# Pooled attention and two feed-forward layers: VectorE shares the pooling of the second batch, and the first block's second product runs unsplit in all sixteen steps

## Chip, cores and metric

The kernel runs on one core of a Trainium2 chip. The metric is the device time of one execution in microseconds; lower is better. The engines are named as in the profile: PE (TensorE, matrix products), PEld (its weight loads), DVE (VectorE), ACT (ScalarE), POOL (GpSimd) and SP (SyncE, whose queue SPq issues the DMAs here). "Lnnn" is line nnn of the kernel before.

## What is computed

Pooled attention over 8 batches of 8 heads, then two feed-forward layers on the 4608 tokens (576 for each batch) of width 512, with an inner width of 2048. All inputs and the output are float32.

```python
k_p = k.reshape(B, H, Sp, pool, D).mean(axis=3)      # pool 8: 576 -> 72
v_p = v.reshape(B, H, Sp, pool, D).mean(axis=3)
scores = scale * np.matmul(q, k_p.transpose(0, 1, 3, 2))
attn = softmax(scores)
x = np.matmul(attn, v_p)                             # then heads side by side: 4608 x 512
h = x @ moe_w_in
g = np.where(h >= 1, h, np.where(h <= -1, 0, (h + 1) ** 2 / 4))
x = g @ moe_w_out
h = x @ moe2_w_in
return np.maximum(h, 0) ** 2 @ moe2_w_out
```

## The kernel before

**Blocks and steps.** The tokens are cut into nine blocks of 512 (`TB`) and 36 attention tiles of 128, four tiles to a block. In the first layer a block takes 16 steps, one for each slice of 128 of the inner width. In step s, `gemm1(s)` (L666) makes the slice's inner values ph from the block's x with 12 matrix products, `step_ops` turns ph into g, and `gemm2(s - 2)` multiplies the g of two steps before (`LAG` is 2) with a slice of `w_out` and adds into four banks acc (L727 or L738). The first block is steps 0 to 15. Its products of step s - 2 are issued right behind the first products of step s.

**Split and unsplit products.** A float32 product is made either from two parts of each operand, a high and a low one, with three products on the parts (hi x hi, hi x lo, lo x hi; `split_hi` on ACT at L219, `split_lo` on DVE at L223), or as one plain float32 product on the operands as they are. `whole("o", s)` chooses the plain form for the second product of the steps below `WHOLE`, 10 before the change. In a plain step there are four products and g is written to a tile that the trace calls gw (L699). In a split step there are twelve products, and besides them wohi (ACT, L219), wolo (DVE, L223), gh (ACT, L701) and gl (DVE, L707).

**Weights.** In the first block the weights of the first layer also arrive (st) and go through a conversion, `convert_w`: two instructions on ACT, three on DVE (L155, L158, L161), one on POOL (L164). There are 16 wi and 16 wo conversions. The program lets them run ahead of their use: behind step s, 2s + 8 are begun (`LEAD` is 8), and they are ended in the step after; 2s + 4 are ended ahead of the g of step s.

**Attention beside the steps.** The attention of the later tiles is cut into small units that are laid into half-steps (`slots`). The first four tiles, those of block 0, are done ahead of step 0. For each batch there are four k tiles and four v tiles of 72 rows by 2 heads by 8 x 64 values (`load_kv`, three buffers kv). `pool_kv` adds the eight positions of a group on DVE in halves (widths 4D and 2D, then the last one, L297 and L298) for batches 2 to 7. The first two batches (`ON_PE` is 2) are summed in the matrix products that also turn k (`unit_k`, products pk, L309) and that place v (`unit_v`, products pv, L329): for batch 1 these go through all eight positions; for batch 0 DVE first adds two halves (L286), and the products go through two positions. Batch 1 is first used by attention tile 4; its units stand in half-steps 2, 3 (k) and 7, 9 (v). The product px (L488) gives a tile of x; it needs the transposed weights of attention aT, which DVE makes (L478) from z, a tile that was stored to DRAM (pd) and fetched back.

**Order.** Every engine works through its own queue in order. The framework sets the order of each queue from the order of the program and the time at which it reckons an operand to be ready, so that a step's instructions can stand among those of a later one: in the trace two pk groups of the program's neighbouring half-steps stand 13 us apart, and some conversions run several steps early. All DMAs stand in the one queue of SP.

Of the kernel before, what the change touches and what calls it, by code (L numbers as in the profile page):

```python
# [21 lines left out]
LEAD = 8  # L22
HEADS = 3

WHOLE = 10

TURNED = 8

# [5 lines left out]
def pooled_attention_moe_moe(  # L34
# [15 lines left out]
    POOL = 8  # L50
# [44 lines left out]
    ON_PE = 2  # L95
# [136 lines left out]
    def bank(shape, name):  # L232

        n = early[-1] % 8 if early else 0
        if n >= 4:
            return ps_acc.tile(shape, F32, tag=f"acc{n - 4}", name=name)
        if n % 2:
            return ps_h.tile(shape, F32, tag="h", name=name)
        return ps_a.tile(shape, F32, tag="a", name=name)
# [39 lines left out]
        kv_t[nm, b, p] = a  # L279

    def pool_kv(nm, b, p):
        if b == 0:

            a = kv_t[nm, b, p]
            for w in (4 * D, 2 * D):
                nc.vector.tensor_tensor(out=a[:, :, 0:w], in0=a[:, :, 0:w], in1=a[:, :, w:2 * w], op=ALU.add)  # L286
        if b < ON_PE:
            return
        a = kv_t.pop((nm, b, p))
        if nm == "v":  # L290
            if p == 0:
                vp[b] = at.tile([SP, H, D], F32, tag="vp", name="vp")
            o = vp[b][:, 2 * p:2 * p + 2, :]
        else:
            o = kp[b, p] = at.tile([SP, 2, D], F32, tag="kp", name="kp", bufs=4)
        for w in (4 * D, 2 * D):
            nc.vector.tensor_tensor(out=a[:, :, 0:w], in0=a[:, :, 0:w], in1=a[:, :, w:2 * w], op=ALU.add)  # L297
        nc.vector.tensor_tensor(out=o, in0=a[:, :, 0:D], in1=a[:, :, D:2 * D], op=ALU.add)  # L298

    def unit_k(b, p0):  # L300
        pk = bank([P, 2, SP], "pk")
        for i in range(2):
            if b < ON_PE:

                a = kv_t.pop(("k", b, p0 + i)).rearrange("s h (r d) -> s h r d", r=POOL)
                n = 2 if b == 0 else POOL
                for r in range(n):
                    for e in range(2):
                        nc.tensor.matmul(  # L309
                            out=pk[e * D:(e + 1) * D, i, :], lhsT=a[:, e, r, :], rhs=ident[:SP, :SP],  # L310
                            start=(r == 0), stop=(r == n - 1),
                        )
                continue
            nc.tensor.transpose(out=pk[:, i, :], in_=kp.pop((b, p0 + i)), identity=ident[:SP, :SP])

        def evac():
            t = kbd[b % 2]
            nc.scalar.activation(out=t[0:D, p0:p0 + 2, 0:SP], in_=pk[0:D], func=AF.Copy)
            nc.scalar.activation(out=t[D:P, p0:p0 + 2, SP:2 * SP], in_=pk[D:P], func=AF.Copy)

        return evac

    def unit_v(b, p0):
        pv = bank([P, 2, 2, D], "pv")
        for i in range(2):
            a = kv_t.pop(("v", b, p0 + i)).rearrange("s h (r d) -> s h r d", r=POOL)
            n = 2 if b == 0 else POOL
            for r in range(n):
                nc.tensor.matmul(  # L329
                    out=pv[:SP, i], lhsT=ident[:SP, :SP], rhs=a[:, :, r, :],  # L330
                    start=(r == 0), stop=(r == n - 1),
                )

        def evac():
            if p0 == 0:
                vp[b] = at.tile([SP, H, D], F32, tag="vp", name="vp")
            nc.scalar.activation(
                out=vp[b][:, 2 * p0:2 * p0 + 4, :], in_=pv[:SP].rearrange("s i h d -> s (i h) d"), func=AF.Copy
            )

        return evac
# [173 lines left out]
    for t in range(TB0, NTILE):  # L515
# [10 lines left out]
        if t in first_tile:  # L526
            b = first_tile.index(t)
# [24 lines left out]
    def pool_to(n):  # L552
        while kv_pooled[0] < min(n, len(kv_order)):
            load_kv_to(kv_pooled[0] + 1)
            pool_kv(*kv_order[kv_pooled[0]])
            kv_pooled[0] += 1
            load_kv_to(kv_pooled[0] + (1 if kv_pooled[0] > 3 * NP else 2))
# [6 lines left out]
    def unit(u):  # L564
        if u[0] == "k":
            b, p = u[1:]
            pool_to(b * 2 * NP + p + 2)
            return unit_k(b, p)
        if u[0] == "v":
            b, p = u[1:]  # L570
            pool_to(b * 2 * NP + NP + p + 2)
            return unit_v(b, p)
        if u[0] == "q":
            load_q_to(u[1] + (1 if u[1] >= TB0 else 0))
            return unit_q(u[1])
        if u[0] == "s":
            return unit_s(*u[1:])
        if u[0] == "p":
            return unit_p(*u[1:])
        b = max(r[2] for r in runs(u[1] * P, P))  # L580
        pool_to((b + 1) * 2 * NP)
        return unit_x(u[1])
# [43 lines left out]
    def whole(kind, s):  # L626

        return kind == "o" and s < WHOLE

# [470 lines left out]
    for n, u in enumerate(units):  # L1100
        kind, b, i, g = u
# [52 lines left out]
```

## Time and profile before

| | us |
|---|---|
| median of three runs | 1641.57 (1641.28 to 1642.41) |
| profiled execution | 1640.99 |
| its span in the trace | 1639.2 |
| PE busy in the span | 1611.4 |
| DVE busy in the span | 1266.7 |

Busy times are sums of the durations of an engine's instructions. In the timelines the duration of a matrix product reaches over the start of the next one; how fast they follow each other is read from their start times. A plain float32 product stands in the trace as two records, as do those of pk and pv. The granted clock is given as a share of TensorE's full clock, 2.4 GHz.

### The profile page before, as it was taken

What the parts mean: (1) busy time and instruction counts of PE and PEld (TensorE: products, weight loads), DVE (VectorE), ACT (ScalarE), POOL (GpSimd) and SP (SyncE); (2) the same over time, 40 slices, a digit from 0 to 9 for tenths busy, and PEclk for the clock granted to TensorE, in tenths of its full rate; (3) what the DMA queues carried; (4) which work ended last, traced back from release to release, by engine and by line L of the source; (5) the groups of instructions that cost most, each with busy time, mean ns of one, the idle gap of its engine ahead of it and who ended that gap; (6) DMA issues with size and microseconds to landing.
All of it is one profiled execution on the core that took longest, in us unless ns stands there. A gap on an engine that the chain in (4) does not pass through costs nothing.

```text
span 1639.2 us, 23215 instructions
## 1 busy us (share of the span) xinstructions
PE 1611.4 (98%) x7776; PEld 1309.5 (80%) x7776; DVE 1266.7 (77%) x2236; ACT 893.4 (55%) x1610; POOL 104.1 (6%) x75
## 2 busy tenths in 40 slices
PE   6999999999999999999999999999999999999998
PEld 5667887888878888888888888888888878888886
DVE  7999889898898999998885452579558855975585
ACT  6665556666666666666775532345435533553353
POOL 1441000001000100000100000000000000000000
PEclk9999999999999999999999999999999999999999
DMA  9665336455454554454370284677777776768675
GB/s 243 187 190 132 87 86 178 140 154 154 133 163 138 168 148 135 149 152 161 129 270 7 96 275 148 194 218 207 194 255 218 209 229 213 211 199 246 193 207 130
DMA packets 280518, 284.69 MB, mean 174 GB/s; under 512 B 154960, under 2 KB 183632, under 8 KB 280400
## 3 DMA queue, kind: packets, MB, share of 16 engines
q1 hardware_dynamic: 280400, 283.21, 58.0%
q8 instruction: 62, 1.02, 0.3%
q14 instruction: 56, 0.46, 0.1%
HBM read 218.10 MB, written 65.01 MB: 173 GB/s over the span
## 4 chain that ended last, share of the span: by engine, by line
PE 92%; DVE 3%; DMA 2%; ACT 1%; issue 1%; SPq 0%; DVEq 0%; ACTq 0%
PE ph L666 26%; PE acc L738 25%; PE dp L1012 11%; PE cp L1003 10%; PE dq L1012 5%; PE cr L1003 5%; PE dr L1012 3%; PE cq L1003 3%; PE pss L372 2%; PE px L488 2%; DMA kv<-in_v_dram 1%; DMA st<-in_moe_w_out_dram 1%; PE acc L727 0%; DMA kv<-in_k_dram 0%; DVE wilo L223 0%
## 5 line engine op out<-in xcount | busy, mean ns | idle before, releaser
L666 PE MATMUL ph<-xhi,wihi 128*128 128x512 f32 x576 | 232.0, 403 | 2.0 <-DVE wi L158 1.9
L666 PE MATMUL ph<-xhi,wilo 128*128 128x512 f32 x576 | 226.3, 393 | 0.0
L666 PE MATMUL ph<-xlo,wihi 128*128 128x512 f32 x576 | 226.3, 393 | 0.0
L960 ACT ACTIVATE gh<-g 128x512 fp32r<-128x512 f32 x224 | 139.8, 630 | 153.0 <-DVE g L1029 47.9
L738 PE MATMUL acc<-gh,wohi 128*128 128x512 f32 x536 | 215.6, 402 | 0.0
L738 PE MATMUL acc<-gl,wohi 128*128 128x512 f32 x536 | 209.8, 391 | 0.0
L738 PE MATMUL acc<-gh,wolo 128*128 128x512 f32 x536 | 209.2, 390 | 0.0
L768 DVE TENSOR_TENSOR gl<-g,gh 128x512 fp32r<-128x512 f32 x224 | 150.9, 685 | 47.6 <-ACT gh L960 46.1
L1003 PE MATMUL cp<-x,w 128*128 128x512 f32 x768 | 186.3, 390 | 0.2
L1003 PEld LDWEIGHTS cp<-x,w 128*128 128x128 f32 x768 | 143.9, 188 | 31.3 <-ACT s L1025 1.4
L1012 PE MATMUL dp<-gh,w 128*128 128x512 f32 x512 | 161.5, 389 | 0.0
L219 ACT ACTIVATE wihi<-wi 128x512 fp32r<-128x512 f32 x144 | 90.4, 628 | 110.9 <-PE ph L666 110.0
L223 DVE TENSOR_TENSOR wilo<-wi,wihi 128x512 fp32r<-128x512 f32 x144 | 106.3, 738 | 43.8 <-ACT wihi L219 42.8
L666 PEld LDWEIGHTS ph<-xhi,wihi 128*128 128x128 f32 x576 | 109.2, 190 | 29.4 <-issue 3.2
L701 ACT ACTIVATE gh<-g 128x512 fp32r<-128x512 f32 x134 | 84.2, 628 | 82.0 <-DVE g L699 80.9
L666 PEld LDWEIGHTS ph<-xhi,wilo 128*128 128x128 f32 x576 | 109.0, 189 | 23.4 <-issue 0.2
L666 PEld LDWEIGHTS ph<-xlo,wihi 128*128 128x128 f32 x576 | 109.2, 190 | 22.0 <-issue 0.7
L707 DVE TENSOR_TENSOR gl<-g,gh 128x512 fp32r<-128x512 f32 x150 | 105.9, 706 | 23.1 <-ACT gh L701 20.1
L1025 ACT ACTIVATE s<-cp 128x512 f32<-128x512 f32 x96 | 57.1, 595 | 118.0 <-PE cp L1003 118.0
L738 PEld LDWEIGHTS acc<-gl,wohi 128*128 128x128 f32 x536 | 100.6, 188 | 22.2
L738 PEld LDWEIGHTS acc<-gh,wohi 128*128 128x128 f32 x536 | 100.7, 188 | 20.2 <-issue 0.8
L738 PEld LDWEIGHTS acc<-gh,wolo 128*128 128x128 f32 x536 | 100.8, 188 | 19.5
(142 smaller groups left out, 2997.3 us busy)
## 6 DMA issues: line engine op xcount, KB each, us to landing
w<-w2i SPq DMA_DIRECT2D x224, 256.0 KB
w<-w2o SPq DMA_DIRECT2D x224, 256.0 KB
w2i<-cb SPq DMA_DIRECT2D x32, 512.0 KB
w2o<-cb SPq DMA_DIRECT2D x32, 512.0 KB
st<-in_moe_w_out_dram SPq DMA_DIRECT2D x31, 512.0 KB
st<-in_moe_w_in_dram SPq DMA_DIRECT2D x29, 512.0 KB
pd<-pad SPq DMA_DIRECT2D x32, 384.0 KB
z<-pd SPq DMA_DIRECT2D x96, 128.0 KB
```

Source lines behind the costliest of these rows:

```text
L219: nc.scalar.activation(out=hi, in_=src, func=AF.Copy)
L223: eng.tensor_tensor(out=lo, in0=src, in1=hi.bitcast(F32), op=ALU.subtract)
L372: nc.tensor.matmul(out=pss[off:off + n, i, :], lhsT=qT[t][:, p, off:off + n], rhs=kbd[b % 2][:, p, :], start=True, stop=True,)
L666: nc.tensor.matmul(out=ph, lhsT=a[:, kk % a.shape[1], :], rhs=c[:, kk, :], start=(i == 0), stop=(i == 3 * KD - 1))
L701: act(out=gh, in_=g, func=AF.Copy)
L707: nc.vector.tensor_tensor(out=gl, in0=g, in1=gh.bitcast(F32), op=ALU.subtract)
L738: nc.tensor.matmul(out=o, lhsT=lhsT, rhs=rhs, start=(f == 0 and x == 0), stop=(f == KF - 1 and x == 2),)
L768: tt(out=out, in0=a, in1=b, op=ALU.subtract)
L960: act(out=hi, in_=a, func=AF.Copy)
L1003: nc.tensor.matmul(out=out[0], lhsT=w[:, a, k, :], rhs=xq[b, i][c][:, k, :], start=(n == 0 and i in (1, 2, 7)), stop=(n == 5), skip_group_ ...
L1012: nc.tensor.matmul(out=out[d], lhsT=w[:, a, d, :], rhs=x[c], start=(g == 0 and n == 0 and i in (1, 2, 7, 4)), stop=(g == NG - 1 and n == 2 ...
L1025: act(out=snaps[key], in_=a, func=AF.Copy)
```

## The change

`WHOLE` goes from 10 to 16, so that the second product of every step of the first block takes the plain float32 form. In `pool_kv`, `unit_k` and `unit_v` the condition `b == 0` becomes `b < ON_PE`: batch 1 is treated as batch 0 is, with two adds on DVE for each of its eight tiles, and products over two positions instead of eight.

```diff
-WHOLE = 10
+WHOLE = 16
     def pool_kv(nm, b, p):
-        if b == 0:
+        if b < ON_PE:
             a = kv_t[nm, b, p]
             for w in (4 * D, 2 * D):
                 nc.vector.tensor_tensor(out=a[:, :, 0:w], in0=a[:, :, 0:w], in1=a[:, :, w:2 * w], op=ALU.add)
     def unit_k(b, p0):
-                n = 2 if b == 0 else POOL
+                n = 2 if b < ON_PE else POOL
     def unit_v(b, p0):
-            n = 2 if b == 0 else POOL
+            n = 2 if b < ON_PE else POOL
```

## Rows read from the trace of the kernel before

**Rows 1.** Page: busy us (share of the span) and instructions of each engine

```profile
PE 1611.4 (98%) x7776; PEld 1309.5 (80%) x7776; DVE 1266.7 (77%) x2236; ACT 893.4 (55%) x1610; POOL 104.1 (6%) x75
```

**Rows 2.** Page: the chain that ended last, by engine

```profile
PE 92%; DVE 3%; DMA 2%; ACT 1%; issue 1%; SPq 0%; DVEq 0%; ACTq 0%
```

**Rows 3.** Busy time by stretch; columns in the first line, behind the stretch its length

```profile
core 0: us, PE busy (x) PEld busy (x) DVE busy (x) ACT busy (x) POOL busy (x), PEclk, DMA share, GB/s
40.00:140.64 100.64, 94.46 (x536) 63.63 (x535) 99.32 (x167) 61.91 (x114) 40.57 (x27) 0.98 0.66 183
140.64:174.00 33.36, 33.36 (x169) 27.20 (x170) 27.80 (x53) 19.13 (x37) 3.54 (x2) 0.95 0.31 85
300.00:600.00 300.00, 300.00 (x1517) 245.34 (x1515) 272.35 (x535) 194.56 (x359) 25.02 (x14) 1.00 0.51 154
```

**Rows 4.** Chain of waits in order of time, from 139 us: start, duration, what

```profile
139.28 1.23 DVE aT L478
...
140.64 1.09 PE px L488 x16
141.74 4.54 PE ph L666 x12
...
152.22 2.72 PE acc L738 x12
```

**Rows 5.** Timeline of PE: start, duration, engine, line; the pooling of batch 1

```profile
43.45 3.22 PE L309 MATMUL pk<-ident,kv 72*64 72x72 f32 x96
46.61 0.50 PE L666 MATMUL ph<-xhi,wihi 128*128 128x512 f32 x1
...
66.78 3.66 PE L329 MATMUL pv<-kv,ident 72*72 72x128 f32 x32
70.20 0.48 PE L666 MATMUL ph<-xhi,wihi 128*128 128x512 f32 x1
```

**Rows 6.** Timeline of PE: an unsplit second product and what follows it

```profile
83.84 3.60 PE L727 MATMUL acc<-gw,wo 128*128 128x512 f32 x8
87.27 0.65 PE L372 MATMUL pss<-kbd,qT 128*128 128x144 f32 x4
```

**Rows 7.** Timeline of DVE: adds of pooling, gl and wolo after the conversions

```profile
168.48 0.68 DVE L297 TENSOR_TENSOR kv<-kv 72x512 f32<-72x512 f32 x1
169.08 0.68 DVE L707 TENSOR_TENSOR gl<-g,gh 128x512 fp32r<-128x512 f32 x1
169.68 0.41 DVE L297 TENSOR_TENSOR kv<-kv 72x256 f32<-72x256 f32 x1
170.01 0.68 DVE L223 TENSOR_TENSOR wolo<-wo,wohi 128x512 fp32r<-128x512 f32 x1
170.62 0.28 DVE L298 TENSOR_TENSOR vp<-kv 72x128 f32<-72x128 f32 x1
```

**Rows 8.** Groups of DVE instructions, 40 to 140.5 us: count, busy us, mean ns

```profile
L297 DVE TENSOR_TENSOR kv<-kv 72x256 f32<-72x256 f32 x4 | 3.6, 906 | 0.1
...
L707 DVE TENSOR_TENSOR gl<-g,gh 128x512 fp32r<-128x512 f32 x2 | 1.4, 684 | 0.0
...
L223 DVE TENSOR_TENSOR wolo<-wo,wohi 128x512 fp32r<-128x512 f32 x2 | 1.4, 677 | 0.0
```

**Rows 9.** Busy time by stretch of L161 alone, a conversion's last DVE instruction

```profile
0.00:85.10 85.10, 14.19 (x18) 0.96 0.81 216
...
0.00:139.20 139.20, 23.31 (x30) 0.98 0.76 201
```

**Rows 10.** Chain of waits (a load of v); waits of SP's queue, total and count

```profile
72.05 7.17 DMA kv<-in_v_dram
79.26 1.97 PE pv L329 x16
...
SPq L128 <- DVE wi L161: 16.4, 8, 3.9
```

**Rows 11.** Timeline of DVE: the g of step 13

```profile
148.99 0.67 DVE L699 SCALAR_TENSOR_TENSOR g<-ph,u 128x512 f32<-128x512 f32 x1
```

## The prediction

> **What bounds the kernel now.** I read four views: shares by engine, the chain of waits, busy time by stretch, and then the timelines of TensorE (PE) and VectorE (DVE) in the first 180 us, where the change lies. The reader is to see that there are two stretches with different bounds. Over the span PE is busy 1611.4 us and DVE 1266.7 us [rows 1], and the chain that ended last is PE for 92% [rows 2]. From 140.64 us on PE has no gap: it is busy 33.36 of 33.36 us up to 174 us, and further in 300 of 300 us from 300 to 600 [rows 3]. There a microsecond of PE work is a microsecond of time, and DVE work is free. Between 40 and 140.64 us the picture turns: DVE is busy 99.32 of 100.64 us, PE 94.46 [rows 3]. PE idles there only some 6 us, so the two engines are close to level, but DVE is the one with nothing left. The last place where PE waits for DVE is the product px of the seventh attention tile, at 140.64 us, which stood behind a transpose that DVE began at 139.28 us [rows 4]; DVE had no pause ahead of it, although the chain lists a DMA just before. From then on PE sets the time. So the sum has two terms: by how much px moves, and how much PE work is added behind it.
>
> **Pooling, the TensorE part.** Batch 1 has four k and four v tiles. Today PE adds eight slices of each. 96 records of pk, three tiles, take 43.45 to 46.61 = 3.16 us, so four take 4.2; 32 records of pv, two tiles, take 66.78 to 70.20 = 3.42 us, so four take 6.8 [rows 5]. Two slices of eight stay: 3/4 of 11.0 us, 8.3 us, leave PE, all of it ahead of 81 us and thus in the stretch where DVE is full.
>
> **Pooling, the VectorE part.** Each of the eight tiles gets one add of 72x512 and one of 72x256. The same shapes stand in the trace for later batches: from 168.48 to 169.08 = 0.60 us and from 169.68 to 170.01 = 0.33 us, to the start of the next instruction [rows 7]. That is 8 x 0.93 = 7.4 us onto DVE, in steps 1 to 4, from roughly 40 to 80 us. A dearer bound: beside the conversions of the weights, where POOL works too, the 72x256 add took 906 ns in the mean instead of 0.41 us [rows 8], which for eight tiles is 8 x 0.5 = 4.0 us more. I take 7.4, because the number of POOL instructions doesn't change, and one of them that stops an add doesn't stop another instruction; the upper end of the range keeps the 4.0. The Trainium skill ("SBUF — State Buffer", section "Who interferes with whom") says that a VectorE instruction with two SBUF inputs and a GpSimd instruction that reads SBUF shut each other out for the whole instruction. The trace agrees with it in the 906 against 412 ns; by that rule with every 72x256 add hit the sum would be the upper end.
>
> **Unsplit product, steps 10 to 15.** Four plain float32 products take the place of twelve split ones. On PE an unsplit step lasts 83.84 to 87.27 = 3.43 us [rows 6], a split one 2.72 us [rows 4]: +0.71 us for each step, 4.3 us for six. The step 10 product stands ahead of px; the other five, 3.5 us, stand behind it and go straight into the time. By the Trainium skill ("FP8 and Floating Point Precision", section "TensorE Precision Notes") true FP32 is four passes, so an unsplit step would be 4/3 of a split one, 3.63 us and +0.91 us, and the six would be 5.4 us. The row's 3.43 us decides.
>
> Off DVE go wolo and gl, 0.61 and 0.60 us of issue each [rows 7], for six steps 7.3 us; off ScalarE go wohi and gh. Only what lies ahead of 139.28 us can bring px forward: two wolo and two gl [rows 8], 2.4 us. The other 4.8 us fall where PE is the bound, and are worth nothing. ScalarE's gain is priced at nothing as well: it is busy 61.91 of 100.64 us [rows 3]. If its cover were gone there would be no loss either, since it only loses work.
>
> **The first term.** Up to 139.28 us DVE gets +7.4 - 2.4 = +5.0 us, with 100.64 - 99.32 = 1.3 us of idle time to put it in. What can give way is work that DVE does early. The program asks for 2s+4 conversions of weights ahead of g of step s. Counting the last instruction of a conversion, 18 are done at 85.1 us, just ahead of g of step 5, which needs 14, and 30 at 139.2 us [rows 9], where the transpose, which the program puts in step 11 behind its first conversion, needs 27. So three are early there. The instruction that I counted takes 23.31/30 = 0.78 us in the mean [rows 9]; a conversion has three such, so 2.3 us at most, and three deferred ones would free up to 7 us. That bounds the shift of px: +5.0 us if the order keeps them ahead, 5.0 - 7 - 1.3 = -3.3 us if all are put off and all idle time is filled. Conversions run early where PE, busy with pooling, left DVE time for them; now PE pools less and DVE more, so some will be put off, and I see no reason for all. I take the middle of 0 and 5.0, **+2.5 us**, since zero already needs more than half of the early ones given up. What is late next in that case is the same transpose, then px.
>
> **The second term** is +3.5 us. The conversions put off then run under gapless PE: g of step 13 came at 148.99 us [rows 11] and its product only after that of step 12 at 152.22 and one more first product, so there is cover of several microseconds, and 1.2 us per step is freed.
>
> **Waits added and queues.** The adds sit on DVE's in-order queue; behind one that waits for its load stand g, wilo and the conversions, and for these PE and the loads wait. No DMA is added, but a kv buffer now comes free after two adds and two slices instead of eight slices. The loads stand in SP's single queue behind loads of weights, which waited for DVE's conversions 16.4 us in eight places, and the last v load took 7.17 us [rows 10]. I price this at nothing in the sum, because an engine that is behind reaches the add later than the load lands, and keep it as a rival.
>
> **Sum.** +2.5 + 3.5 = +6.0 us on the profiled execution's 1640.99 us is 1647.0. The median of the runs is 1641.57, 0.6 us above that, so 1647.6 us. The forecast's own range is a shift of 0 to +5.0: 1645.1 to 1650.1.
>
> **The rivals.**
> (a) TensorE is the bound all along, and the early conversions absorb everything: px moves with PE's own work. Then PE loses 8.3 and gains 4.3 us: 1637.6 us, **faster**. For it: PE stood without a gap over long pieces of the stretch, and idled only 6 us in all. Against it: it would take 7 or more us out of a DVE that idles 1.3 us. It decides once all three early conversions and more are put off. Chance 0.15.
> (b) The early conversions absorb the adds but no more: px moves by -3.3 to -0.2 us, the five unsplit steps remain; +0.2 to +3.3, about 1643.4 us, no change that can be measured. This is also what is left if the order of work comes out different but equal in worth. Chance 0.20.
> (c) DVE stops for a load of kv. Priced by the last v landing, 7.17 us [rows 10], half of it to all of it on top of the forecast's upper half (+6.0 to +8.5): 1651 to 1657 us. For it: PE itself waited for a v load at 79.26 us in the chain. Against it: only the last tiles are loaded that late. Chance 0.12.
> That the change doesn't do what it says has nothing for it: both conditions are plain comparisons.
>
> **How the numbers follow.** Forecast 0.53, (a) 0.15, (b) 0.20, (c) 0.12. About 0.2%, 3.3 us, is what a measurement of this kernel can tell from no change. Faster is (a), 0.15. Same is (b) and 0.02 of the forecast's low edge, 0.22. Slower is the rest, 0.63. The range of 8 in 10 runs from (a), 1637.5, to the forecast's upper end with the 4.0 us of dearer adds, 1654: it leaves out half of (a) and part of (c).
>
> **What would show it.** Right: between 40 and 140 us DVE still full and PE's idle time up from 6 to 14 us or more; pooling products down to a quarter; px of the seventh tile 0 to 5 us later than 140.64; behind it gapless PE with five unsplit steps of 3.43 us. The first step is wrong if px comes earlier: then (a) or (b), told apart by how much, and by the count of conversions done ahead of it (27 or 28 instead of 30). (c) would show as idle DVE with a kv load as what ended it. Wrong in another way would be a stretch of lower granted clock behind a longer idle time of PE: after the 1.9 us wait at 140.64 the twelve products of the first product took 4.54 instead of 2.72 us [rows 4]; one more such stretch costs up to 1.8 us.

## The result and the profile after

The changed kernel takes 1655.32 us (median of 6 runs, 1653.57 to 1656.75), the kernel before 1641.42 us in the same comparisons: ratio 1.008, 95% interval 1.007 to 1.009, 13.9 us slower. The forecast was 1647.6 us with a range up to 1654.0. The direction was right; the size was more than twice the +6 us that was forecast, and outside the range.

The profiled execution took 1656.18 us. Page, engines' busy time:

```profile
span 1654.4 us, 22876 instructions
PE 1612.4 (97%) x7608; PEld 1299.0 (79%) x7608; DVE 1263.9 (76%) x2240; ACT 884.9 (53%) x1598; POOL 109.2 (7%) x75
```

Both totals are nearly those of [rows 1], while the span grew by 15.2 us. The time went into waits and into slower products, not into work. Busy time by stretch, columns as in [rows 3]:

```profile
40.00:120.85 80.85, 64.78 (x299) 39.30 (x297) 78.41 (x136) 47.23 (x88) 41.13 (x22) 0.98 0.67 176
120.85:174.00 53.15, 53.15 (x206) 33.26 (x207) 38.13 (x74) 22.56 (x43) 10.64 (x7) 0.93 0.50 129
300.00:600.00 300.00, 298.71 (x1534) 244.14 (x1533) 272.56 (x529) 192.74 (x356) 24.09 (x14) 1.00 0.50 147
```

Up to the last of its early waits for DVE, now at 120.85 us and not at 140.64, PE idles 16 us instead of the 6 of [rows 3], and DVE is as full as before. And from 300 to 600 us, where PE had no gap before, it has one of 1.3 us. The pooling products, timeline of PE, as in [rows 5], are as short as forecast, one of them waiting for its add:

```profile
73.02 0.63 PE L329 MATMUL pv<-kv,ident 72*72 72x128 f32 x4 [0.38 <-ACT wo L150]
75.59 3.60 PE L727 MATMUL acc<-gw,wo 128*128 128x512 f32 x8
81.13 0.66 PE L329 MATMUL pv<-kv,ident 72*72 72x128 f32 x4 [1.95 <-DVE kv L286]
```

**Where the 15 us arise.** ACT's first instruction on ph (u, L689) comes once in each step of the first layer, so the difference of its start times in two traces shows how late a step is. Timeline of ACT, steps 24 and 142, of the kernel before and then of the changed one:

```profile
213.36 0.58 ACT L689 ACTIVATE u<-ph 128x512 f32<-128x512 f32 x1
919.06 0.60 ACT L689 ACTIVATE u<-ph 128x512 f32<-128x512 f32 x1 [2.03 <-PE ph L666]
```

```profile
219.94 0.58 ACT L689 ACTIVATE u<-ph 128x512 f32<-128x512 f32 x1
933.31 0.60 ACT L689 ACTIVATE u<-ph 128x512 f32<-128x512 f32 x1 [2.03 <-PE ph L666]
```

At step 24 the changed kernel is 6.58 us late: I call this the **near shift**. At step 142 it is 14.25 us late: 7.67 us more, the **far shift**, which arises hundreds of microseconds behind the last instruction that the diff touches. (The remaining 0.9 us, to 15.2, come in the second layer.) Single steps jump by some us where an engine does its attention work in another order; the shift is read where it stays level. The far shift has two visible places, the second and third of these waits of PE for DVE in the timeline of the changed kernel; the kernel before has none of the three:

```profile
120.85 1.98 PE L488 MATMUL px<-aT,vp 72*64 72x128 f32 x16 [7.34 <-DVE sm L433]
...
472.67 1.09 PE L488 MATMUL px<-aT,vp 72*64 72x128 f32 x16 [1.29 <-DVE aT L478]
...
694.81 1.55 PE L488 MATMUL px<-aT,vp 72*64 72x128 f32 x12 [3.16 <-DVE aT L478]
```

All three are px waiting for the transposed weights aT. The first is the near one, at the sixth attention tile, one tile ahead of where the forecast looked. (Its releaser is the transpose, which ran from 119.47 to 120.70 us; the instruction named started just before its end.)

**How aT gets late, far.** DVE makes aT when its queue comes to it. The chain of waits of the changed kernel, ahead of the far wait at 694.81 us, tells what its queue stood behind:

```profile
680.62 4.29 DMA st<-in_moe_w_in_dram
684.93 0.67 ACT z L150
685.62 0.43 DVE z L155
...
693.51 1.16 DVE aT L478
694.68 0.14 issue
694.81 1.98 PE px L488 x16
```

The transfer at its head is a load of weights of the second layer, which go through the conversion in these steps. (The z of L150 and L155 is a tile of the conversion, and not the fetched z.) It was issued at 680.62 us and landed 4.29 us later; ACT had stood idle for it 2.54 us, and DVE 2.50 us for ACT. From 685.62 us to the transpose DVE had no pause, so it was not the fetch of z that it waited for. Ahead of the load stands a row of loads of q. Timeline of SP, first the kernel before at the same tile, then the changed one:

```profile
659.64 2.34 SPq L754 DMA_DIRECT2D x2t<-o  x3
662.03 3.87 SPq L255 DMA_DIRECT2D q<-in_q_dram  x8
666.00 0.39 SPq L128 DMA_DIRECT2D st<-in_moe_w_in_dram  x1
666.49 0.45 SPq L613 DMA_DIRECT2D pd<-pad  x1
```

```profile
671.00 1.31 SPq L754 DMA_DIRECT2D x2t<-o  x3
672.37 8.16 SPq L255 DMA_DIRECT2D q<-in_q_dram  x16
680.62 0.39 SPq L128 DMA_DIRECT2D st<-in_moe_w_in_dram  x1
681.11 0.45 SPq L613 DMA_DIRECT2D pd<-pad  x1
```

The queue issues a load of q in 0.5 us. Before, eight of them stand ahead of the load of weights and of the store of pd behind it, now sixteen, and that row takes 4.3 us longer. No line of that stretch was changed; the framework's order of SP's queue came out different.

**How aT gets late, near.** Here the store of pd came late too: DVE wrote that pad from 90.99 us, and it was stored at 101.53 us; in the kernel before it was written from 93.69 us and stored at 95.13. But that was not what px waited for. The fetch of z was issued at 106.73 us, and from there to the transpose at 119.47 us DVE was busy without a pause, mostly with conversions. Busy time by stretch, and the transpose in the timeline of DVE:

```profile
106.73:119.47 12.74, 4.87 (x16) 2.17 (x14) 12.74 (x20) 5.66 (x11) 5.16 (x4) 0.94 0.88 215
```

```profile
119.47 1.23 DVE L478 STREAM_TRANSPOSE aT<-z 96x1024 f32<-96x1024 f32 x1
```

So the near wait is DVE being late with its own work, and the far one is SP's queue, by way of ACT and DVE.

### The profile page after: what moved, and what is told of

It is laid out like the page before. It is cut to its first block, busy times and chain, and to the rows that moved or that the text cites. A ratio compares the mean times of both kernels' runs of the same rounds, so it can differ in the third digit from the quotient of the medians.

```text
span 1654.4 us, 22876 instructions
## 1 busy us (share of the span) xinstructions
PE 1612.4 (97%) x7608; PEld 1299.0 (79%) x7608; DVE 1263.9 (76%) x2240; ACT 884.9 (53%) x1598; POOL 109.2 (7%) x75
## 4 chain that ended last, share of the span: by engine, by line
PE 66%; DVE 2%; DMA 1%; SPq 1%; ACT 0%; issue 0%; DVEq 0%; ACTq 0%
PE acc L738 15%; PE ph L666 14%; PE dp L1012 11%; PE cp L1003 10%; PE dq L1012 5%; PE cr L1003 5%; PE dr L1012 3%; PE cq L1003 3%; PE px L488 1%; PE pss L372 1%; DMA w<-w2i 1%; SPq L255 0%; DMA st<-in_moe_w_in_dram 0%; DVE g L699 0%; DVE aT L478 0%
## 5 line engine op out<-in xcount | busy, mean ns | idle before, releaser
L960 ACT ACTIVATE gh<-g 128x512 fp32r<-128x512 f32 x224 | 139.5, 630 | 151.4 <-DVE g L1029 48.0
L738 PE MATMUL acc<-gh,wohi 128*128 128x512 f32 x512 | 206.2, 403 | 0.0
L738 PE MATMUL acc<-gl,wohi 128*128 128x512 f32 x512 | 200.1, 391 | 0.0
L738 PE MATMUL acc<-gh,wolo 128*128 128x512 f32 x512 | 199.7, 390 | 0.0
L768 DVE TENSOR_TENSOR gl<-g,gh 128x512 fp32r<-128x512 f32 x224 | 151.0, 686 | 47.7 <-ACT gh L960 46.0
L223 DVE TENSOR_TENSOR wilo<-wi,wihi 128x512 fp32r<-128x512 f32 x144 | 102.7, 713 | 45.9 <-ACT wihi L219 44.8
L701 ACT ACTIVATE gh<-g 128x512 fp32r<-128x512 f32 x128 | 80.5, 629 | 78.6 <-DVE g L699 78.2
L707 DVE TENSOR_TENSOR gl<-g,gh 128x512 fp32r<-128x512 f32 x144 | 100.7, 699 | 23.5 <-ACT gh L701 20.9
L738 PEld LDWEIGHTS acc<-gl,wohi 128*128 128x128 f32 x512 | 96.1, 188 | 21.3
L738 PEld LDWEIGHTS acc<-gh,wohi 128*128 128x128 f32 x512 | 96.3, 188 | 19.8 <-issue 0.8
L1012 PEld LDWEIGHTS dp<-gh,w 128*128 128x128 f32 x512 | 96.1, 188 | 19.9
```

The source lines that it names most:

```text
L223: eng.tensor_tensor(out=lo, in0=src, in1=hi.bitcast(F32), op=ALU.subtract)
L701: act(out=gh, in_=g, func=AF.Copy)
L707: nc.vector.tensor_tensor(out=gl, in0=g, in1=gh.bitcast(F32), op=ALU.subtract)
L738: nc.tensor.matmul(out=o, lhsT=lhsT, rhs=rhs, start=(f == 0 and x == 0), stop=(f == KF - 1 and x == 2),)
L768: tt(out=out, in0=a, in1=b, op=ALU.subtract)
L960: act(out=hi, in_=a, func=AF.Copy)
```

## The experiments

The theory after this reading (A): the near shift is VectorE's adds and the unsplit steps; the far shift is the changed order of SP's queue. Rivals: the unsplit steps cause it all (B); the pooling causes it all (C); the far waits are of another origin (D). The table has all runs; near and far shift are measured as above against the first trace of the kernel before. "q loads" is how many loads of q stand in SP's queue between the store of x2t near 660 us and the next store of pd, with the time from the one to the other; the load of weights named above stands behind the same row. c1, c2, e6, e7 and e8 were timed once. The last column is PE's wait for aT near 690 us.

| run | steps unsplit | adds of batch 1 | positions in products | time us (before beside it) | near | far | q loads | wait us |
|---|---|---|---|---|---|---|---|---|
| before | 10 | none | 8 | 1641.42 | 0 | 0 | 8, 6.9 us | 0 |
| c1_before | 10 | none | 8 | 1642.82 (1642.52) | +2.2 | 0.0 | 8, 6.6 us | 0 |
| changed | 16 | all | 2 | 1655.32 (1641.42) | +6.6 | +7.7 | 16, 10.1 us | 3.16 |
| c2_after | 16 | all | 2 | 1655.88 (1642.52) | +5.9 | +7.8 | 16, 10.3 us | 3.56 |
| e1_whole16 | 16 | none | 8 | 1641.34 (1643.36) | +4.0 | 0.0 | 5, 6.1 us | 0 |
| e4_whole13 | 13 | none | 8 | 1640.16 (1643.36) | +2.4 | 0.0 | 4, 6.3 us | 0 |
| e2_pool1 | 10 | all | 2 | 1660.89 (1643.36) | +11.0 | +10.7 | 19, 11.0 us | 3.40 |
| e7_short_only | 10 | none | 2 | 1654.82 (1641.34) | +2.9 | +11.3 | 20, 11.6 us | 3.67 |
| e3_no_adds | 16 | none | 2 | 1648.82 (1643.36) | -0.5 | +5.1 | 17, 11.1 us | 3.31 |
| e8_adds_only | 16 | all | 8 | 1652.03 (1641.34) | +12.2 | 0.0 | 2, 6.1 us | 0 |
| e9_v_only_16 | 16 | v | k 8, v 2 | 1649.83 (1642.52) | +5.9 | 0.0 | 10, 6.8 us | 0 |
| e10_v_only_10 | 10 | v | k 8, v 2 | 1660.70 (1642.52) | +11.4 | +7.8 | 19, 11.7 us | 2.27 |
| e5_after_pd_act | 16 | all | 2 | 1648.04 (1641.34) | +9.1 | 0.0 | store on ACT | 0 |
| e6_before_pd_act | 10 | none | 8 | 1644.10 (1641.34) | +2.9 | 0.0 | store on ACT | 0 |

**Two traces of one kernel.** No edit in either.

> The kernel before once more, for a second trace: how far shifts of the start of u between two traces of one kernel go without any change. Expected: under 1 us up to step 142 if the shifts are the program's; 2 us or more if chips or executions differ that much, and then near shifts of that size mean nothing.

> The changed kernel once more, for a second trace beside the one above. Theory A: near shift +6.6 us and far shift +7.7 us within 1 us each, px waits for aT at the sixth tile (7.3 us), near 473 (1.3 us) and near 695 us (3.2 us) again. A rival by which the far waits are chance of one execution: they are gone or elsewhere.

The second trace of the kernel before is 2.2 us late at step 24, where under 1 us was expected; it was 0.6 us late at step 2 and 3.7 at step 4, and nothing is added behind step 24. So executions differ in the near part, and a near shift read from one trace is known to 2 or 3 us only. Some traces were also taken of executions off their kernel's median: those of e1 and e4 2.9 and 3.2 us above it, those of e3 and e9 2.7 and 2.8 us below. A second estimate of the near shift, from ratio of times less far shift, is -1.3 us for e1, -2.6 for e4, +1.0 for e3, +7.5 for e2 and +5.5 for the changed kernel. The changed kernel repeats its near shift within 0.7 us and its far shift within 0.1, with waits at the same places (5.64, 1.57 and 3.56 us). The far waits belong to the program, not to one execution.

**Unsplit steps alone.**

```diff
-WHOLE = 10
+WHOLE = 16      # e1; 13 in e4
```

> Only WHOLE goes to 16; pooling stays as before. Read is the start of u (L689) of steps 24 to 34 against the kernel before (the near shift, +6.58 us in the changed kernel), and what is added after that (the far shift, +8.6 us there, with waits of px for aT near 473 and 695 us). Theory A (the near shift is five unsplit steps behind the last wait of px, 3.5 us, and VectorE's adds for the rest; the far shift is a different order of work planned for the later steps): near shift +0.5 to +3.6 us, since two wolo and two gl leave VectorE ahead of px; a far shift of 0 to +8 us that need not have waits at the same places. Rival B (the unsplit steps cause it all): near +6 us, far +8 us at the same two places. Rival C (the pooling causes it all): time within 2 us of before.

> The kernel before with WHOLE 13 instead of 10: three more unsplit steps, pooling as before. Theory A: near shift between -1.5 and +1.5 us (two steps behind px at 0.71 us, less what VectorE saves ahead of it); and, since the order of all later work is planned anew, a far shift that is not proportional to the number of unsplit steps: waits of px for aT at other places than in the kernel with 16, or none. A rival in which the far shift is carried by the first block's delay: far shift between that of before (0) and that of WHOLE 16, with waits at the same places.

No far shift in either, which ends rival B. The near shifts, +4.0 and +2.4 us, are a little above what was expected of A, and no more than 2 to 3 us sure. The times themselves show no difference for 16 (ratio 0.9992, 0.9978 to 1.0007) and a gain at the edge of what can be told for 13 (0.9984, 0.9973 to 0.9995). The traces, one for each kernel, point the other way; I take both as not clearly different from before. In the trace of e1 px no longer waits at 140 us, where the kernel before lost 1.90 us and in its first trace 1.8 us more in slower products [rows 4], together about what five unsplit steps cost; instead PE waits 1.85 us for a load of v at 81.07 us.

**Pooling alone.**

```diff
-        if b == 0:                          # pool_kv
+        if b < ON_PE:
-                n = 2 if b == 0 else POOL   # unit_k, unit_v
+                n = 2 if b < ON_PE else POOL
```

> Only the pooling of batch 1 is changed; WHOLE stays 10. Theory A: VectorE gets the adds, 13 us busy in the changed kernel's trace, and no relief ahead of the first waits of px; the near shift is +1 to +5 us, with a wait of px for aT between 100 and 145 us of 4 us or more; far shift 0 to +8 us, by the order that is planned. Rival B (the unsplit steps cause it all): TensorE loses 8.3 us, time at or under before. Rival C (the pooling causes it all): near +6 us, far +8 us.

Ratio 1.0111 (1.0095 to 1.0127): slower than both parts together. Near +11.0 us, well above A's +1 to +5: the sixth, seventh and eighth tile's px wait 5.32, 3.16 and 2.69 us. So with the new pooling the unsplit steps help: by 4.4 us near in the traces, and by some 5 us in the times (ratio 1.008 instead of 1.0111, intervals apart). Without it they change nothing that the times show (0.9992). Rival C fails in its numbers, but has the place of the far shift right.

**Adds and short products apart.** e3 and e7 take the adds away and leave the products at two positions; e8 keeps the adds and the eight positions.

```diff
-        if b < ON_PE:                       # pool_kv, e3 (WHOLE 16) and e7 (WHOLE 10)
+        if b == 0:
-                n = 2 if b < ON_PE else POOL   # unit_k and unit_v, e8 (WHOLE 16)
+                n = 2 if b == 0 else POOL
```

> The changed kernel without VectorE's two adds for the tiles of batch 1: the products still go over two positions, so six of eight positions of batch 1 are left out of the sum. TensorE's work is that of the changed kernel, VectorE's is less by the 16 adds. Theory A (VectorE is the bound from 40 to 140 us and the adds make the near shift): the wait of px of the sixth tile (7.3 us in the changed kernel) is gone or under 2 us, and the near shift falls from +6.6 to between -4 and +1 us. A rival in which the adds are beside other work (a load of kv, the latency of the store and fetch of z): the wait and the near shift stay within 2 us of +6.6.

> WHOLE 10 and no adds, but the products of batch 1 over two positions (six of eight left out of the sum): TensorE's relief alone. Measured so far in near shifts: unsplit steps alone +4.03 us, unsplit and short products -0.47 us, all three +6.58 us. If the terms add, short products alone give -4.5 us near; theory A expects less gain, -4 to +1 us, since VectorE then also keeps the wolo and gl of steps 10 to 15. Far shift: if it goes with the short products (all three kernels with them had a px wait of 3.2 to 3.4 us near 690 us, the two without had none), +4 us or more; if it is a matter of chance in the planned order, any value.

> WHOLE 16 and VectorE's adds for batch 1, but the products still go over all eight positions (positions are thus counted more than once): VectorE's cost alone on top of unsplit steps. If the terms add: near shift +4.03 + 7.05 = +11.1 us. Theory A: +9 to +13 us, since TensorE, which then has nothing taken off, stands with VectorE in the same stretch. A rival in which the adds cost time only because TensorE has got ahead of VectorE: +4 to +7 us. Far shift: near 0 if it goes with the short products.

With these the near shift can be split, to 2 or 3 us. The adds cost 7.0 us (e3 to changed), 8.1 (e7 to e2) and 8.2 (e1 to e8) in the traces, the same in all three settings as far as that tells; by the second estimate the first of these is 4.5 us. The wait that makes the cost differs: in e8, whose +12.2 us was expected at 9 to 13, it is one of 8.25 us ahead of a pv product at 89.57 us, for an add. The short products gain 4.5 us (e1 to e3) and 5.6 (e8 to changed) with unsplit steps in the traces; by the times e1 to e3 is no gain but a loss of some 2 us, so that their gain is not shown. Without unsplit steps they bring nothing (e7, +2.9 us where -4 to +1 was expected): px waits 4.83, 1.54 and 2.69 us for aT near 114, 144 and 165 us. e3's wait at the sixth tile was expected to fall under 2 us and stayed at 4.29: A was wrong there, DVE is too late for the faster PE even without the adds. Stretches of e7 up to its first such wait, columns as in [rows 3]:

```profile
40.00:100.00 60.00, 55.34 (x270) 34.95 (x269) 58.44 (x97) 39.36 (x75) 25.29 (x19) 1.00 0.68 201
100.00:114.10 14.10, 9.27 (x37) 5.60 (x36) 14.03 (x24) 6.64 (x13) 5.92 (x5) 0.91 0.72 194
```

DVE is full, 14.03 of 14.10 us, while PE has 4.8 us to spare: 8 us less PE work buys nothing where DVE doesn't follow. The far shift comes with short products only (changed, e2, e3, e7, e10), and not in the runs without them, with unsplit steps (e1, e4) or with unsplit steps and adds (e8). In all six traces that have the wait near 690 us ACT waits 1.2 to 2.9 us for the load of weights behind the row of q; in those without it, with the store on SP, only in e4 (1.5 us). In e2, e7 and e10 px also waits near 255, 305 and 750 us (0.3 to 1.5 us), which their far shifts hold too; these waits were not followed back.

**v tiles alone.**

```diff
-        if b == 0:                                       # pool_kv
+        if b == 0 or b < ON_PE and nm == "v":
-            n = 2 if b == 0 else POOL                    # unit_v only
+            n = 2 if b < ON_PE else POOL
```

> The change with the k tiles left as before: only the four v tiles of batch 1 get adds and short products; WHOLE 16. VectorE gets half of the adds (about 6 us busy) and saves 7.3 us, TensorE saves 5.1 us ahead of 81 us and gets 4.3. Theory A (VectorE is the bound in the stretch, TensorE's relief there isn't paid): near shift +1.5 to +4.5 us, that is unsplit steps alone (+4.0) within 2.5 us. If instead TensorE's relief counts: -3 us or less. Far shift: with fewer short products ahead of it, 0 if a wait of px near 690 us is missing, 4 us or more if at least 16 loads of q stand between the store of x2t near 660 us and the next store of pd.

> As the run above with WHOLE 10: half of the adds and 5.1 us of TensorE's relief, no relief of VectorE. Short products alone gave +2.9 us near, short products with all adds +11.0. Theory A: near shift between them, +3 to +8 us, slower than its counterpart with WHOLE 16. If TensorE's relief counts: -3 us or less. Far shift as above, by the number of loads of q between the two stores.

Ratios 1.0033 (1.0002 to 1.0064) and 1.0115 (1.0086 to 1.0145). Both near shifts, +5.9 and +11.4 us, are above the ranges given: with half of the change the near part costs about as much as with all of it. In e10 PE waited 4.85 us ahead of a pv product at 82.62 us, in e9 2.90 and 2.85 us at 78.73 and 88.19, which A had not counted. The far shift went as the queue's order said: 10 loads of q and no wait in e9, 19 and a wait in e10.

**The store of pd off SP's queue.**

```diff
-            nc.sync.dma_start(out=p_d[t], in_=pad[t % 2])
+            nc.scalar.dma_start(out=p_d[t], in_=pad[t % 2])   # e5: on the changed kernel, e6: on the one before
```

> The changed kernel with one difference: the 32 stores of the weights to DRAM (pd from pad, 384 KB each) are issued on ScalarE's queue instead of SP's. Theory A (the far shift of 8 us comes from stores of pd that stand in SP's queue behind a whole tile's 16 loads of q, 8.2 us at 672 us, so that z, aT and px come late): the waits of px for aT near 473 and 695 us are gone, the far shift (from step 34 on) is between -1 and +2 us; the near shift may move by up to 4 us either way, since ScalarE's queue is in order too. Rival D (the far waits come from VectorE's or ScalarE's order, or from the transfers themselves): a far shift of 5 us or more stays.

> The kernel before with the same 32 stores on ScalarE's queue, as the counterpart to the run above: what the move does by itself. Theory A: within 4 us of the kernel before, with no px wait behind 200 us. If it is slower by 6 us or more, the move costs ScalarE too much, and the run above must be read against this one.

The far shift is gone: 0.0 us, no px wait behind 200 us, and the changed kernel falls from 1655.3 to 1648.0 us, ratio to before 1.0035 (1.0015 to 1.0054). The same tile as above, timelines of SP, ACT's queue and PE of e5:

```profile
667.50 0.43 SPq L128 DMA_DIRECT2D st<-in_moe_w_in_dram  x1
668.71 1.31 SPq L754 DMA_DIRECT2D x2t<-o  x3
670.08 7.89 SPq L255 DMA_DIRECT2D q<-in_q_dram  x12
```

```profile
676.98 0.37 ACTq L613 DMA_DIRECT2D pd<-pad  x1
```

```profile
692.27 1.09 PE L488 MATMUL px<-aT,vp 72*64 72x128 f32 x16
```

The store comes at 676.98 us, 4.1 us ahead of the changed kernel's 681.11, and px doesn't wait. But the move made the order of SP's queue anew as well: the load of weights now stands ahead of the row of q, 13.1 us earlier than in the changed kernel. So e5 shows that the far shift hangs on the order of SP's queue, and not that it is the store; by the chain above it is the load, so that the transfers and the waits of ACT and DVE, which rival D names, are part of the cause. No run moves the load alone or changes the length of the row alone. The near shift did not fall: +9.1 us; the move by itself shows +2.9 us in the one trace of e6, hardly more than two traces of the kernel before differ by. Near, the wait went from one tile to the next:

```profile
117.48 1.09 PE L488 MATMUL px<-aT,vp 72*64 72x128 f32 x16 [0.79 <-DVE pn L397]
...
145.57 1.76 PE L488 MATMUL px<-aT,vp 72*64 72x128 f32 x14 [4.39 <-DVE aT L478]
```

## Why the prediction was wrong

**The bound.** "DVE is the one with nothing left" between 40 and 140 us held, and is what the near shift rests on: DVE was full up to the transpose that px waited for, and the adds cost 7.0 to 8.2 us in the traces in every setting in which they were put in or taken out.

**The TensorE part of the pooling.** Its size was right (four pv records take 0.39 us of PE before the next product starts where sixteen took 1.7), but it was entered in the sum at nothing, as work beside a full DVE. Together with unsplit steps the traces have it giving back 4.5 to 5.6 us, which the times don't bear out; without them it gave back nothing.

**The adds.** Forecast 7.4 us, with 4.0 us more as the dearer bound. Groups of DVE in the changed kernel, 40 to 140 us, columns as in [rows 8]:

```profile
L286 DVE TENSOR_TENSOR kv<-kv 72x512 f32<-72x512 f32 x8 | 9.0, 1128 | 0.0
L286 DVE TENSOR_TENSOR kv<-kv 72x256 f32<-72x256 f32 x8 | 4.2, 530 | 0.0
```

13.2 us busy, at the dearer bound and beyond: the 72x512 adds, 0.68 us long in [rows 7], took 1.13, as the Trainium skill's rule on the shared port ("SBUF — State Buffer", "Who interferes with whom") allows for any of them. What they cost in time was 4 to 8 us all the same: the reason given, that a POOL instruction which stops an add stops nothing else, fits, but was not tested by itself.

**The first term, +2.5 us, failed in its reason.** I let deferred conversions absorb half of the adds. Hardly anything was absorbed: ahead of the sixth tile's transpose 25 conversions were done where the kernel before had 26, the transpose started at 119.47 instead of 112.40 us, and px of that tile came at 120.85 instead of 118.06 us behind a wait of 7.34 us. The order of DVE's queue is fixed ahead of time and DVE works through it as it stands; that this kept the conversions early fits, but no run tested it. The wait also came one tile ahead of where I looked. Px of the seventh tile was to come 0 to 5 us later; it came 11 us later, without a wait. Timeline of PE, the kernel before and then the changed one:

```profile
140.64 1.09 PE L488 MATMUL px<-aT,vp 72*64 72x128 f32 x16 [1.90 <-DVE aT L478]
```

```profile
151.60 1.09 PE L488 MATMUL px<-aT,vp 72*64 72x128 f32 x16
```

The 1.90 us that the kernel before waited there, and 1.8 us of slower products behind it in its first trace, were gone, and the sum had not counted on that.

**The second term, +3.5 us.** Unsplit steps took 3.0 to 3.4 us, where 3.43 was read in [rows 6]. Of the changed kernel,

```profile
135.22 3.60 PE L727 MATMUL acc<-gw,wo 128*128 128x512 f32 x8
138.25 0.79 PE L666 MATMUL ph<-xhi,wihi 128*128 128x512 f32 x1
```

has the next product 3.03 us after, another pair 3.44 us. The size for each step is about right. As a term of the time it is not shown: e1 and e4 have +4.0 and +2.4 us near in their traces and no loss in their times. That what the unsplit steps save was "worth nothing" behind px was wrong where the pooling is in: there it paid 3.4 to 4.4 us in the traces, net of the steps' cost. Whether that is VectorE's part or ScalarE's, which the forecast priced at nothing too, was not tested apart.

So the near sum, +6.0 forecast and +6.6 measured (+5.9 in the second trace), came out right by luck: the wait was at another tile, the adds cost more than the +2.5 us that the first term left of them, and what set that off, a wait that fell away and perhaps the short products, was not in the sum.

**The step that failed for good is the end of the sum**: "From then on PE sets the time". It was true of the kernel before, and I carried it to the changed one as if the order of all later work were given. The order of SP's queue was made anew for the whole program and put sixteen loads of q instead of eight ahead of a load of weights at 680.62 us; ACT, DVE and then px began to wait in a stretch without spare time. That is the missing 7.7 us, which the sum had at nothing for that sentence's sake; in e5, where the load stands ahead of the row, it is gone. The chain was read for the wait at 694.81 us, which is worth 6.3 of the 7.7. The one at 472.67 us, 1.29 us long, also follows on a conversion of weights of the second layer; its chain was not followed back to a row of loads. None of the rivals had it: (c) saw the danger in SP's queue, but only for loads of kv and only near the change. What stays open is why the order comes out so with short products; the traces show that it does, in five kernels with at least the v products short and the store on SP, and not in the sixth (e9).

**The other rivals.** (a), faster by PE's own work, and (b) did not occur; e3, with neither adds nor split steps, is what (a) would have needed, and had a near shift of -0.5 us. (c) did not occur: DVE's idle time up to 120 us is not ended by a load of kv.

## What to carry to other kernels

Where a framework orders the queues from the whole program, a local change can move a transfer in a stretch that it doesn't touch; so look in the trace of before for the places where a latency chain (here load, conversion on ACT and DVE, transpose, product) has only a few microseconds to spare behind a row of loads on a shared queue, and leave room for them in the range. After the run, plot the shift of one instruction that comes once per step: it tells in one look whether a loss arises at the change or elsewhere. Then follow the chain back from the wait before naming a cause: a store that came late here was not what the engine waited for. And where two engines are level, price the parts of a change together: here the same edit changed nothing measurable alone and saved some 5 us beside the other.

## What the runs showed of the hardware

A wait of PE can cost more than its length. Behind the 7.34 us at 120.85 us the twelve products of the next first product took 5.29 us instead of 2.88 in the kernel before, and the granted clock was 0.50, the lower of the two levels, 1.2 GHz, from 120.85 to 127 us. Behind the 3.16 us at 694.81 us it was 0.50 up to 700 us, and 0.70 in the mean up to 706; behind the 1.29 us at 472.67 us it stayed at 1.00. Waits of one length need not end alike: in the kernel before the 1.90 us ahead of 140.64 us were followed by 0.70 up to 146.3 us, in its second trace 1.93 us ahead of 143.72 us by 1.00 up to 150. Busy time by stretch of the changed kernel:

```profile
694.80:706.00 11.20, 11.19 (x47) 9.11 (x48) 8.41 (x17) 5.53 (x11) 1.30 (x1) 0.70 0.20 41
472.60:484.00 11.40, 11.33 (x62) 9.38 (x63) 10.69 (x23) 7.81 (x15) 0.57 (x1) 1.00 0.58 181
```

So the far wait of 3.16 us is worth 6.3 us in the shift of u (from +7.9 at step 86 to +14.3 at step 106), and the one of 1.29 us about 1.4 (from +6.6 at step 55).
